# Attention scores in 64 x 64 quarters of the array, keys of the second batch prepared earlier in the step, and averages of v by TensorE

## The chip, the cores and the metric

The kernel runs on one core of a Trainium2 chip. The metric is the time of one execution in microseconds (us) on the device. One execution was also profiled; its trace gives the span from the first to the last instruction and every row shown below. The engines are called as the profile calls them: PE is TensorE's products and PEld its loads of the stationary operand, DVE is VectorE, ACT ScalarE, POOL GpSimd, and SP the engine that issues the DMA transfers.

## What is computed

Three parts stand one behind the other. All of it is float32.

```python
# attention: 2 batches, 8 heads, 768 positions, head size 64, block 32, window 16
k_sum = k.reshape(B, H, 24, 32, D).max(axis=3)
v_sum = v.reshape(B, H, 24, 32, D).mean(axis=3)
mask_l = abs(pos[:, None] - pos[None, :]) < 16
scores = concat(where(mask_l, scale * q @ k.T, -1e9), scale * q @ k_sum.T + log(32))
a = softmax(scores)
x = a @ concat(v, v_sum)
# dense MLP, 1536 tokens: 512 -> 2048 -> 512
h = x @ w_in
x = (h * sigmoid(h)) @ w_out
# top-1 mixture of 8 experts, 512 -> 1024 -> 512, capacity 384
out[i] = gate[i] * (relu(x[i] @ w1[e]) @ w2[e])
```

## The kernel before

The order of the instructions on every engine is the order in which the code is written; nothing reorders it.

**Units.** The attention is cut into 24 units of 256 queries and one pair of heads: four pairs per block of queries (`NPAIR` = 4), three blocks per batch, so twelve units per batch (`NPB`). A window of 96 keys (`WL`) and the 24 block keys make 120 columns (`WK`) for each group of 64 queries (`QB`), and a unit has four such groups (`UB`).

**Step.** `attn_step(n)` issues one step, in which several units are at different stages: maxima of unit n-1 (`s_max`, DVE), product with v of unit n-3 (`a_mm`, PE), transposes of P of unit n-2 (`p_mm`, PE), exponentials of n-1 (`s_exp`, ACT), transposes of queries of n+1 (`q_mm`, PE), copies of the attention's output of n-3 (`x_hi` on ACT, `x_lo` on DVE), copies out of the transposes (`p_ev`, `q_ev`), normalisation of n-1 (`s_norm`, DVE, then POOL), and at the end the scores of unit n (`s_mm`, PE). From unit 7 on a step begins with the MLP's first product for an earlier block (`l1`, L451), and from unit 9 it also has a second product (`l2_to`, L481) ahead of the scores. Pieces of the conversion of the MLP's weights (`conv_part`: three operations on DVE, a cast on ACT at L436, a subtraction on POOL at L437) stand between the stages.

**Scores before.** The queries of a unit lie transposed in `qt`. `q_ev` (L287) copies them with four ACT copies of 64 x 128 into `qbd`, a block-diagonal tile (two heads, each 64 rows by 64 columns, zero elsewhere), which POOL clears once at the start (L129). `s_mm` (L294) then needs four products, one for each group of 64 queries, which use the whole array and give 128 rows: 64 queries of one head above 64 of the other.

**Keys.** `k_prep(b, p)` transposes the keys of a pair of heads (L242) into two PSUM banks, `kA` and `kB`, ACT copies the windows out of them into `kwin` (L257, L261), and DVE takes the maxima of blocks of 32 (L263). It runs for the first batch ahead of the first scores (steps -1 to 2), and for the second in steps 11 to 14, behind the second product of the MLP and directly ahead of the scores.

**Averages of v.** For the first batch TensorE makes them: `vsum_mm(0)` multiplies v by a matrix `avg` of 1/32 (L207), behind the first scores, and ACT copies the result to `vsum` (L211), from where DMAs put rows of it to each unit's v (L343). For the second batch they are summed in steps 3 to 11: eight loads (`load_vs`), additions on POOL for three of them (L219, L221), reductions on DVE for five (L223), two more to bring parts together, and eight small DMAs that place them (`vs_place`).

**PSUM.** Of the eight banks, the pool "att" has four, which `qt`, `kA`, `kB`, `sc`, `pt`, `av` and `vsp` take in turn; "h" (first product) and "x2" (second) have two each.

## Time and profile before

| what | value |
|---|---|
| median of 3 runs | 515.15 us (514.3 to 515.69) |
| the profiled execution | 514.7 us |
| span of its trace | 513.0 us |
| mean granted TensorE clock | 0.976 of full |
| PE busy | 479.9 us |
| DVE busy | 296.0 us |
| ACT busy | 247.4 us |
| POOL busy | 135.6 us |

A median is compared with a median; the rows of the trace belong to the one profiled execution and are taken against its span of 513.0 us, which lies 1.7 us under that execution's time. Busy times of engines lie beside each other and do not add up.

### The profile page before, as it was taken

Reading aid. Unit: us, or ns where it says so; the run is one execution under the profiler, and the core shown is the slowest. Engines: PE = TensorE matmul, PEld = TensorE weight load, DVE = VectorE, ACT = ScalarE, POOL = GpSimd, SP = SyncE. Lnnn points to the kernel's source line nnn. Section 1 sums busy time; section 2 is a strip of 40 time slices with the busy share of each in tenths; the row PEclk is TensorE's granted clock in tenths of the full one; section 3 lists DMA queues with packets and bytes.
Section 4 is the critical chain, followed back from the end, with each engine's and each line's share of the span. In section 5 each row is a group of like instructions: output and inputs, shape, how many; then the busy total and the mean of one; then the engine's idle time right before and its main releaser. Section 6 shows DMA issues by size and latency. Waiting matters only on the chain. (4 is left out here: it accounts for less than half of the span.)

```text
span 513.0 us, 9798 instructions
## 1 busy us (share of the span) xinstructions
PE 479.9 (94%) x3318; PEld 416.8 (81%) x3318; DVE 296.0 (58%) x857; ACT 247.4 (48%) x746; POOL 135.6 (26%) x154
## 2 busy tenths in 40 slices
PE   4877989999999999999999999999999998999994
PEld 2366878898988899999998998888878897988852
DVE  1277886765545988666666434556666673445500
ACT  4478868977753533333333333334543344346511
POOL 6027753362433532222112100112412012101011
PEclk9957989999999999999999999999999999999998
DMA  8479777246301677655540000128251367718470
GB/s 204 101 201 278 187 193 200 65 121 165 75 2 42 173 211 215 217 156 149 151 177 0 1 1 0 44 74 318 78 191 55 89 204 226 251 45 288 151 236 16
DMA packets 82055, 71.15 MB, mean 139 GB/s; under 512 B 36822, under 2 KB 66776, under 8 KB 81984
## 3 DMA queue, kind: packets, MB, share of 16 engines
q1 hardware_dynamic: 80288, 66.17, 44.6%
q0 software_dynamic: 1696, 4.13, 2.1%
q8 instruction: 33, 0.54, 0.4%
q14 instruction: 38, 0.31, 0.2%
HBM read 55.38 MB, written 15.09 MB: 137 GB/s over the span
## 5 line engine op out<-in xcount | busy, mean ns | idle before, releaser
L451 PE MATMUL hp<-xT,w 128*128 128x256 f32 x1152 | 156.8, 286 | 2.3 <-ACT w L436 1.4
L451 PEld LDWEIGHTS hp<-xT,w 128*128 128x128 f32 x1152 | 149.6, 192 | 8.1 <-ACT w L436 1.6
L481 PE MATMUL x<-w,g 128*128 128x512 f32 x576 | 151.6, 398 | 1.1 <-ACT rows L487 1.1
L481 PEld LDWEIGHTS x<-w,g 128*128 128x128 f32 x576 | 101.8, 189 | 20.2 <-issue 2.1
L454 ACT ACTIVATE u<-hp 128x256 f32<-128x256 f32 x96 | 37.0, 385 | 98.3 <-PE hp L451 94.8
L459 DVE SCALAR_TENSOR_TENSOR u<-u,hp 128x256 f32<-128x256 f32 x96 | 40.2, 418 | 63.9 <-ACT u L454 63.6
L463 ACT CAST g<-u 128x256 fp32r<-128x256 f32 x96 | 39.4, 410 | 60.3 <-DVE u L459 60.0
L437 POOL TENSOR_TENSOR w<-cv,w 128x512 fp32r<-128x512 f32 x32 | 42.8, 1339 | 95.9 <-ACT w L436 95.8
L791 PE MATMUL hp<-XT,H 128*128 128x384 f32 (+1 forms) x288 | 48.8, 320 | 2.2 <-ACTq L948 1.4
L791 PEld LDWEIGHTS hp<-XT,H 128*128 128x128 f32 x288 | 45.8, 188 | 4.6 <-ACTq L948 1.8
L757 PE MATMUL y<-H,gh 128*128 128x512 f32 x192 | 48.6, 397 | 0.0
L467 DVE TENSOR_TENSOR g<-u,g 128x256 fp32r<-128x256 f32 x72 | 31.4, 437 | 27.6 <-ACT g L463 17.0
L326 POOL TENSOR_TENSOR P<-P,rs 128x480 f32<-128x480 f32 x24 | 26.3, 1095 | 60.6 <-DVE rs L325 53.8
L757 PEld LDWEIGHTS y<-H,gh 128*128 128x128 f32 x192 | 35.1, 188 | 7.2 <-issue 0.4
L736 DVE TENSOR_TENSOR H<-R,H 128x1024 fp32r<-128x1024 f32 x24 | 29.4, 1224 | 17.2 <-ACT H L735 17.2
L568 POOL DMA_INDIRECT disp<-rows,di x12 | 13.4, 1119 | 97.5 <-DVE rows L566 58.7
L316 ACT ACTIVATE P<-P,nm 128x120 f32<-128x120 f32 x96 | 36.6, 384 | 4.2 <-DVE nm L305 4.1
L796 ACT ACTIVATE gh<-hp 128x384 fp32r<-128x384 f32 (+1 forms) x24 | 10.9, 456 | 47.2 <-PE hp L791 46.7
L294 PEld LDWEIGHTS sc<-kwin,qbd 128*128 128x128 f32 x192 | 28.3, 220 | 4.8 <-DVE nm L305 1.7
L294 PE MATMUL sc<-kwin,qbd 128*128 128x120 f32 x192 | 30.2, 308 | 2.0 <-DVE nm L305 1.0
L735 ACT CAST H<-R 128x1024 fp32r<-128x1024 f32 x27 | 28.1, 1042 | 2.2 <-SPq L948 1.6
L765 POOL DMA_INDIRECT out_dram<-ys,aux x8 | 9.8, 1231 | 72.2 <-ACT ys L764 36.5
(175 smaller groups left out, 576.7 us busy)
## 6 DMA issues: line engine op xcount, KB each, us to landing
R<-in_moe_w_dram SPq DMA_DIRECT2D x34, 512.0 KB
ri<-in_moe_w_in_dram SPq DMA_DIRECT2D x16, 512.0 KB
ro<-in_moe_w_out_dram SPq DMA_DIRECT2D x16, 512.0 KB
disp<-zt SPq DMA_DIRECT2D x24, 260.0 KB
q_n<-in_q_dram SPq DMA_DIRECT2D x48, 64.0 KB
k_n<-in_k_dram SPq DMA_DIRECT2D x16, 192.0 KB
out_dram<-zt SPq DMA_DIRECT2D x12, 256.0 KB
rows<-in_moe_w_dram SPq DMA_DIRECT2D x6, 512.0 KB
```

The costliest lines, as they stand in the source:

```text
L294: PE.matmul(sc[:, i, :], lhsT=qbd[u % 2][:, i, :], rhs=kwin[p][:, i0 + i, :], start=True, stop=True)
L316: ACT.activation(P[:, i, :], P[:, i, :], AF.Exp, bias=nm[:, i : i + 1], scale=-1.0, accum_out=sm[:, i : i + 1])
L437: POOL.tensor_sub(w[:, 2 * j + 1, :], t, w[:, 2 * j, :].bitcast(F32))
L451: PE.matmul(hp, lhsT=w[:, a, c], rhs=x[:, b_, kk, :], start=n == 0, stop=n == 3 * KT - 1)
L454: ACT.activation(u, hp, AF.Tanh, scale=0.5)
L459: DVE.scalar_tensor_tensor(out=u, in0=u, scalar=1.0, in1=hp_t.pop(s), op0=ALU.add, op1=ALU.mult)
L463: ACT.copy(gt[s][:, 0, :], u_t[s])
L467: eng.tensor_sub(gt[s][:, 1, :], u_t.pop(s), gt[s][:, 0, :].bitcast(F32))
L481: PE.matmul(x2[blk][t], lhsT=gh[:, a, c], rhs=w[:, b_, :], start=first and n == 0, stop=last and n == 2)
L736: (eng or DVE).tensor_sub(h[:, 1], r, h[:, 0].bitcast(F32))
L757: PE.matmul(y, lhsT=gh[:, a, c], rhs=mx[1, f // 2][:, b_, DM * (f % 2) : DM * (f % 2) + DM], start=first and n == 0, stop=last and n == 2,)
L791: PE.matmul(hp, lhsT=h1(f // 2, a, kk, c), rhs=XT[:, b_, kk, 0:N], start=n == 0, stop=n == 3 * KT - 1)
```

## The change

Four things change.

1. *Scores.* `s_mm` has eight products in place of four. Each multiplies the 64 rows of one head by 64 queries, and so takes one quarter of the array: the head (h) chooses the upper or lower 64 rows, and the even or odd group of queries (e) the columns. The two heads write to two PSUM banks. `qbd` goes; `q_ev` is one copy of 128 x 256 to `qT`. The mask has three groups of columns instead of six. `load_q` reads runs of 256 bytes instead of 512.
2. *A bank of its own.* `qa` is one of the four "att" banks for good: the transposed queries lie in its first half, the product with v in its second. Three are left to take turns for scores (two of them at a time), transposes of P, and the keys of the second batch.
3. *Keys.* `kB` begins at 384 instead of 512, so no window lies across both banks: seven transposes instead of six, four ACT copies instead of eight, and the maxima are issued ahead of the copies. The first batch's keys use the banks "x2"; the second batch's preparation moves ahead of the second product.
4. *Averages of v.* The first batch's product moves from behind the scores of unit 0 to behind those of unit 1, takes a bank of "h", and is copied out by DVE; its loads move behind those of the third keys, and `vs_rows` one step later. The second batch's eight loads, POOL and DVE sums and placing DMAs go. Four loads take their place, each of a pair of heads, and `vs_mm` with six products of 24 x 128 in steps 12, 13, 15 and 16, copied out by DVE.

Constants that only the router needs are set later on POOL (`late_constants`), and the first weights' conversion is begun in steps 3 and 5 instead of 2 and 4.

```diff
+    qa = psum.tile([128, 2, 256], F32, tag="att", bufs=4, name="qa")
...
-    qbd = [ap1.tile([128, UB, 128], F32, name=f"qbd{i}") for i in range(2)]
-    for t in qbd:
-        POOL.memset(t, 0.0)
...
+    VR = S // 128
+    avg6 = ap1.tile([128, VR, NSUM], F32, name="avg6")
+    POOL.memset(avg6, 1.0 / BLK)
+    for sgn in (1, -1):
+        POOL.affine_select(
+            out=avg6,
+            in_=avg6,
+            pattern=[[sgn, VR], [-sgn * BLK, NSUM]],
+            compare_op=ALU.is_ge,
+            fill=0.0,
+            base=0 if sgn == 1 else BLK - 1,
+            channel_multiplier=sgn * VR,
+        )
+    late_constants()
...
-            SP.dma_start(out=t[:, h], in_=q[b, 2 * p + h, s0 : s0 + TB, :].rearrange("(p r) d -> p r d", r=2))
+            SP.dma_start(out=t[:, :, h], in_=q[b, 2 * p + h, s0 : s0 + TB, :].rearrange("(t p) d -> p t d", p=128))
...
-    NVP = 4
-
-    def load_vs(b, i):
-        g, j = divmod(i, NVP)
-        n = BLK // NVP
-        t = stage.tile([96, n, D], F32, tag="vs", bufs=2, name="vs_n")
+    def load_vs(b, p):
+        t = stage.tile([128, 2, VR, D], F32, tag="vs", bufs=2, name="vs_n")
         SP.dma_start(
-            out=t,
-            in_=v[b, 4 * g : 4 * g + 4].rearrange("h (n t) d -> (h n) t d", t=BLK)[:, j * n : j * n + n, :],
+            out=t.rearrange("p h r d -> p h (r d)"),
+            in_=v[b, 2 * p : 2 * p + 2].rearrange("h (p r) d -> p h (r d)", r=VR),
         )
-        vs_n[b, i] = t
+        vs_n[b, p] = t
...
-        ps = psum.tile([128, H, D], F32, tag="att", bufs=4, name="vsp")
+        ps = psum.tile([128, H, D], F32, tag="h", bufs=2, name="vsp")
...
-        ACT.copy(vsum[WL:WK], ps[WL:WK])
-
-    def vs_reduce(b, i):
-        g, j = divmod(i, NVP)
-        t = vs_n.pop((b, i))
-        if i < 3:
-            w = BLK // NVP // 2
-            while w > 1:
-                POOL.tensor_add(t[:, 0:w, :], t[:, 0:w, :], t[:, w : 2 * w, :])
-                w //= 2
-            POOL.tensor_add(vs_p[g][:, j, :], t[:, 0, :], t[:, 1, :])
-        else:
-            DVE.reduce_sum(vs_p[g][:, j, :], t.rearrange("p t d -> p d t"), axis=AX.X)
-        if j == NVP - 1:
-            DVE.reduce_sum(vs_t[g], vs_p[g].rearrange("p j d -> p d j"), axis=AX.X)
-            DVE.tensor_scalar_mul(vs_t[g], vs_t[g], 1.0 / BLK)
-
-    def vs_place():
-        for g in range(2):
-            for h in range(4):
-                SP.dma_start(out=vsum[WL:WK, 4 * g + h, :], in_=vs_t[g][NSUM * h : NSUM * h + NSUM, :])
+        DVE.tensor_copy(vsum[WL:WK], ps[WL:WK])
+
+    def vs_mm(b, p):
+
+        t = vs_n.pop((b, p))
+        ps = psum.tile([128, 2, D], F32, tag="h", bufs=2, name="vs2")
+        for r in range(VR):
+            PE.matmul(ps[WL:WK], lhsT=avg6[:, r, :], rhs=t[:, :, r, :], start=r == 0, stop=r == VR - 1)
+        DVE.tensor_copy(vsum[WL:WK, 2 * p : 2 * p + 2, :], ps[WL:WK])
...
-        c0 = 512
-        pa = psum.tile([128, 512], F32, tag="att", bufs=4, name="kA")
-        pb = psum.tile([128, 512], F32, tag="att", bufs=4, name="kB")
-        for i in range(S // 128):
-            dst = pa[:, 128 * i : 128 * i + 128] if i < 4 else pb[:, 128 * i - 512 : 128 * i - 384]
-            PE.transpose(dst, t[:, i].rearrange("p h d -> p (h d)"), ident)
...
+        parts = []
+        for name, lo, hi, w0, w1_, c in (("kA", 0, 512, 0, 7, 0), ("kB", 384, S, 7, NQB, 512)):
+
+            tag, bufs = ("x2", 2) if b == 0 else ("att", 4)
+            ps = psum.tile([128, 512], F32, tag=tag, bufs=bufs, name=name)
+            for i in range(lo // 128, hi // 128):
+                PE.transpose(ps[:, 128 * i - lo : 128 * i - lo + 128], t[:, i].rearrange("p h d -> p (h d)"), ident)
+            parts.append((ps, lo, hi, w0, w1_, c))
+        for ps, lo, hi, w0, w1_, c in parts:
             DVE.reduce_max(
-                ks[:, lo // BLK : hi // BLK],
-                src[:, 0 : hi - lo].rearrange("p (n t) -> p n t", t=BLK),
+                ks[:, c // BLK : hi // BLK],
+                ps[:, c - lo : hi - lo].rearrange("p (n t) -> p n t", t=BLK),
                 axis=AX.X,
             )
+            i = w0
+            while i < w1_:
+                n = 1
+                while i + n < w1_ and wstart(i + n) == wstart(i) + n * QB:
+                    n += 1
+                a = wstart(i) - lo
+                assert a >= 0 and a + (n - 1) * QB + WL <= hi - lo
+                sl = ps[:, a : a + 1]
+                ACT.copy(
+                    kw[:, i : i + n, 0:WL],
+                    bass.AP(tensor=sl.tensor, offset=sl.offset, ap=[list(sl.ap[0]), [QB, n], [1, WL]]),
+                )
+                i += n
...
-        qt = psum.tile([128, TB], F32, tag="att", bufs=4, name="qt")
+        qt = qa[:, 0]
         t = q_n.pop(u)
-        for h in range(2):
-            PE.transpose(qt[:, 128 * h : 128 * h + 128], t[:, h].rearrange("p r d -> p (r d)"), ident)
+        for i in range(2):
+            PE.transpose(qt[:, 128 * i : 128 * i + 128], t[:, i].rearrange("p h d -> p (h d)"), ident)
         qt_t[u] = qt
 
     def q_ev(u):
-        qt = qt_t.pop(u)
-        for h in range(2):
-            dst = qbd[u % 2][64 * h : 64 * h + 64, :, 64 * h : 64 * h + 64].rearrange("p i (c r) -> p i c r", r=2)
-            for r in range(2):
-
-                src = qt[64 * r : 64 * r + 64, 128 * h : 128 * h + 128]
-                ACT.copy(dst[:, :, :, r], src.rearrange("p (i c) -> p i c", c=QB // 2))
+        q_t[u] = ap2.tile([128, TB], F32, tag="qT", name="qT")
+        ACT.copy(q_t[u], qt_t.pop(u))
...
     def s_mm(u):
         T, p = divmod(u, NPAIR)
         i0 = (T % NTH) * UB
-        sc = psum.tile([128, UB, WK], F32, tag="att", bufs=4, name="sc")
-        for i in range(UB):
-            PE.matmul(sc[:, i, :], lhsT=qbd[u % 2][:, i, :], rhs=kwin[p][:, i0 + i, :], start=True, stop=True)
+
+        sc = [psum.tile([128, UB // 2, WK], F32, tag="att", bufs=4, name="sc") for _ in range(2)]
+        qT = q_t.pop(u)
+        for j in range(UB // 2):
+            for h in range(2):
+                w = slice(D * h, D * h + D)
+                for e in range(2):
+                    i = 2 * j + e
+                    PE.matmul(
+                        sc[h][QB * e : QB * e + QB, j, :],
+                        lhsT=qT[w, QB * i : QB * i + QB],
+                        rhs=kwin[p][w, i0 + i, :],
+                        start=True,
+                        stop=True,
+                    )
         sc_t[u] = sc
...
-        av = psum.tile([128, TB], F32, tag="att", bufs=4, name="av")
+        av = qa[:, 1]
...
-        if n > 1 and (n - 1) % NPB == 0 and n - 1 < NU:
-            vs_place()
         on(p_mm, n - 2)
         conv_part()
         on(g_mul, s, NS)
         on(load_v, n - 1)
-        on(vs_rows, n - 1)
         on(s_exp, n - 1)
         conv_part()
         on(q_mm, n + 1)
         on(x_hi, n - 3)
-        if n == 0:
-            for T in range(NTH):
-                load_vp(0, T)
+        b, r = divmod(n + 1, NPB)
+        if 0 < b < B and r < NPAIR:
+
+            k_prep(b, r)
+        for p, (_, nu) in enumerate(VS_STEPS):
+            if n == nu:
+                vs_mm(1, p)
         l2_to(s - 2)
+        on(vs_rows, n - 2)
         on(p_ev, n - 2)
         on(q_ev, n + 1)
         on(s_norm, n - 1)
@@ -1071,32 +1077,36 @@
         if b < B and r < NPAIR:
             load_k(b, r)
         conv_part()
-        b, r = divmod(n + 8, NPB)
-        if 0 < b < B and r < 2 * NVP:
-            vs_reduce(b, r)
         on(x_lo, n - 3)
         b, r = divmod(n + 1, NPB)
-        if 0 <= b < B and r < NPAIR:
+        if b == 0 and r < NPAIR:
             k_prep(b, r)
         on(g_hi, s, NS)
         if n in (4, 5):
             load_raw()
             load_raw()
-        b, r = divmod(n + 9, NPB)
-        if 0 < b < B and r < 2 * NVP:
-            load_vs(b, r)
+        for p, (nl, _) in enumerate(VS_STEPS):
+            if n == nl:
+                load_vs(1, p)
         on(g_lo, s, NS)
         on(s_mm, n)
         if n == 0:
+            for T in range(NTH):
+                load_vp(0, T)
+        if n == 1:
             vsum_mm(0)
 
     NS = len(steps)
+
+
+    VS_STEPS = ((NPB - 4, NPB), (NPB - 3, NPB + 1), (NPB + 1, NPB + 3), (NPB + 2, NPB + 4))
+    assert B == 2 and len(VS_STEPS) == NPAIR
     fills = []
 
     for n in range(-2, NS + 2 + LEAD):
         s = n - LEAD
         if s < 0:
-            if n in (2, 4):
+            if n in (3, 5):
                 conv_to(n // 2)
             attn_step(n)
             continue
```

The first place is TensorE at the start of the program, from the first scores (`sc` of unit 0) to the third. `qt` and `qa` are transposed queries, `kA` and `kB` transposed keys, `vsp` the first batch's averages of v, `pt` transposes of P, `av` the product with v. Before:

```order
L294 MATMUL sc<-kwin_144,qbd_148 128x120 x4
L207 MATMUL vsp<-vp_n,avg 24x512 x6
L277 MATMUL qt<-ident,q_n 128x128 x2
L242 MATMUL kA<-ident,k_n 128x128 x4
L242 MATMUL kB<-ident,k_n 128x128 x2
L294 MATMUL sc<-kwin_145,qbd_149 128x120 x4
L332 MATMUL pt<-ident,P 120x128 x4
L277 MATMUL qt<-ident,q_n 128x128 x2
L242 MATMUL kA<-ident,k_n 128x128 x4
L242 MATMUL kB<-ident,k_n 128x128 x2
L294 MATMUL sc<-kwin_146,qbd_148 128x120 x4
```

And with the change, on the same engine and stretch:

```order
L291 MATMUL sc<-kwin_126,qT 64x120 x8
L273 MATMUL qa<-ident,q_n 128x128 x2
L243 MATMUL kA<-ident,k_n 128x128 x4
L243 MATMUL kB<-ident,k_n 128x128 x3
L291 MATMUL sc<-kwin_127,qT 64x120 x8
L218 MATMUL vsp<-vp_n,avg 24x512 x6
L336 MATMUL pt<-ident,P 120x128 x4
L273 MATMUL qa<-ident,q_n 128x128 x2
L243 MATMUL kA<-ident,k_n 128x128 x4
L243 MATMUL kB<-ident,k_n 128x128 x3
L291 MATMUL sc<-kwin_128,qT 64x120 x8
```

The averages have moved from ahead of the second unit's queries, keys and scores to behind them, and stand directly ahead of the first transposes of P.

The second place is ACT from the second unit's keys to the first exponentials and the next queries. `kwin` is where the key windows go, `P` the exponentials. Before:

```order
L257 COPY kwin_145<-kB 128x2x96
L261 COPY kwin_145<-kB 128x96
L211 COPY vsum<-vsp 24x512
L316 ACTIVATE P,sm<-P,nm 128x120 x4
L287 COPY qbd_148<-qt 64x4x32 x4
```

With the change:

```order
L278 COPY qT<-qa 128x256
L259 COPY kwin_127<-kA 128x96
L259 COPY kwin_127<-kA 128x6x96
L259 COPY kwin_127<-kB 128x4x96
L259 COPY kwin_127<-kB 128x96
L320 ACTIVATE P,sm<-P,nm 128x120 x4
```

The copy of the averages no longer stands ahead of the first exponentials on this engine.

The third place is TensorE in step 12, a unit with keys of the second batch: `hp` is the MLP's first product, `x` its second, `vs` the averages of the second batch. Before:

```order
L451 MATMUL hp<-xT,w 128x256 x12
L356 MATMUL av<-PT,v_n 64x64 x8
L332 MATMUL pt<-ident,P 120x128 x4
L277 MATMUL qt<-ident,q_n 128x128 x2
L481 MATMUL x_875<-w,g 128x512 x3
L481 MATMUL x_876<-w,g 128x512 x3
L242 MATMUL kA<-ident,k_n 128x128 x4
L242 MATMUL kB<-ident,k_n 128x128 x2
L294 MATMUL sc<-kwin_144,qbd_148 128x120 x4
```

With the change:

```order
L455 MATMUL hp<-xT,w 128x256 x12
L360 MATMUL qa<-PT,v_n 64x64 x8
L336 MATMUL pt<-ident,P 120x128 x4
L273 MATMUL qa<-ident,q_n 128x128 x2
L243 MATMUL kA<-ident,k_n 128x128 x4
L243 MATMUL kB<-ident,k_n 128x128 x3
L229 MATMUL vs_1128<-vs_n,avg_135 24x128 x6
L485 MATMUL x_830<-w,g 128x512 x3
L485 MATMUL x_831<-w,g 128x512 x3
L291 MATMUL sc<-kwin_126,qT 64x120 x8
```

Keys' transposes now stand ahead of the second product, and six products of averages between the two.

## Rows read from the trace of the kernel before

**Rows 1.** Page, part 1: busy time, share of the span, instructions.

```profile
PE 479.9 (94%) x3318; PEld 416.8 (81%) x3318; DVE 296.0 (58%) x857; ACT 247.4 (48%) x746; POOL 135.6 (26%) x154
```

**Rows 2.** Stretches: length; PE, PEld, DVE, ACT, POOL busy; clock, DMA share, GB/s.

```profile
0.00:21.00 21.00, 13.68 (x37) 6.21 (x37) 3.47 (x14) 6.39 (x25) 7.96 (x32) 1.00 0.73 165
21.00:50.40 29.40, 20.91 (x157) 17.79 (x157) 19.81 (x72) 24.74 (x100) 14.07 (x15) 0.73 0.80 216
50.40:74.40 24.00, 20.90 (x183) 18.47 (x182) 20.79 (x69) 17.59 (x67) 14.51 (x16) 0.90 0.76 193
74.40:108.90 34.50, 34.13 (x314) 30.50 (x314) 24.69 (x97) 28.96 (x126) 14.00 (x18) 1.00 0.52 126
108.90:152.90 44.00, 44.00 (x414) 39.69 (x413) 23.30 (x109) 31.42 (x126) 17.41 (x20) 1.00 0.39 94
```

**Rows 3.** Timeline of PE: start, duration, instruction, count; one unit.

```profile
108.93 1.67 PE L451 MATMUL hp<-xT,w 128*128 128x256 f32 x12
...
111.76 1.62 PE L481 MATMUL x<-w,g 128*128 128x512 f32 x6
...
113.23 1.05 PE L294 MATMUL sc<-kwin,qbd 128*128 128x120 f32 x8
...
114.03 0.36 PE L451 MATMUL hp<-xT,w 128*128 128x256 f32 x1
```

**Rows 4.** Timeline around the router's logits.

```profile
312.53 0.16 PEld L508 LDWEIGHTS lt<-xt,wg 128*32 128x32 f32 x8
...
312.53 0.64 PE L508 MATMUL lt<-xt,wg 128*32 128x256 f32 x8
...
313.10 0.50 PE L481 MATMUL x<-w,g 128*128 128x512 f32 x1
```

**Rows 5.** Timeline of PEld: two loads of the first batch's averages.

```profile
17.85 0.10 PEld L207 LDWEIGHTS vsp<-vp_n,avg 128*24 128x24 f32 x1 [0.33 <-issue]
18.28 0.10 PEld L207 LDWEIGHTS vsp<-vp_n,avg 128*24 128x24 f32 x1 [0.33 <-issue]
```

**Rows 6.** Timeline of a unit with keys of the second batch.

```profile
78.67 0.60 PE L242 MATMUL kA<-ident,k_n 128*128 128x128 f32 x4
...
79.11 0.38 PE L242 MATMUL kB<-ident,k_n 128*128 128x128 f32 x2
...
79.33 0.24 ACT L261 COPY kwin<-kA 128x96 f32<-128x96 f32 x1
```

**Rows 7.** Timeline of the start, ACT, PE and DVE; idle before and releaser in brackets.

```profile
8.29 1.14 ACT L287 COPY qbd<-qt 64x128 f32<-64x128 f32 x4 [2.83 <-POOL qbd L129]
...
11.98 0.54 PE L294 MATMUL sc<-kwin,qbd 128*128 128x120 f32 x1
...
13.95 7.07 PE L207 MATMUL vsp<-vp_n,avg 128*24 128x512 f32 x12
...
21.05 0.58 ACT L211 COPY vsum<-vsp 24x512 f32<-24x512 f32 x1 [7.46 <-PE vsp L207]
...
24.89 0.65 PE L332 MATMUL pt<-ident,P 128*120 128x128 f32 x4 [1.88 <-POOL P L326]
...
29.23 1.64 PE L294 MATMUL sc<-kwin,qbd 128*128 128x120 f32 x6 [0.82 <-ACT PT L338]
...
30.06 0.43 DVE L422 TENSOR_SCALAR cv<-ri 128x512 uint32<-128x512 uint32 x1 [2.40 <-DMA ri<-in_moe_w_in_dram]
```

**Rows 8.** Groups, 50.4 to 74.4: count, busy us, mean ns, idle before.

```profile
L451 PE MATMUL hp<-xT,w 128*128 128x256 f32 x49 | 8.3, 320 | 2.3 <-ACT w L436 1.4 <-POOL w L437 0.8
...
L287 ACT COPY qbd<-qt 64x128 f32<-64x128 f32 x17 | 4.6, 272 | 0.3
...
L223 DVE TENSOR_REDUCE vs_p<-vs_n 96x64 f32<-96x512 f32 x4 | 4.2, 1060 | 0.0
...
L369 ACT CAST xT<-av 128x256 fp32r<-128x256 f32 x4 | 1.4, 353 | 0.0
```

**Rows 9.** Timeline of DVE ahead of the first MLP product.

```profile
49.16 1.50 DVE L324 TENSOR_SCALAR rs<-sm 128x4 f32<-128x4 f32 x1 [1.08 <-ACT P L316]
```

More of the change, by code (lines that the diff above doesn't have):

```diff
@@ L106, in big_tile @@
         return big.tile(shape, dtype, tag="big", name=name)
-    mask = ap1.tile([128, 6, WK], F32, name="mask")
+    mask = ap1.tile([128, 3, WK], F32, name="mask")
     POOL.memset(mask, 0.0)
-    for h in range(2):
-        m = mask[64 * h : 64 * h + 64]
-        for lo, hi, off in ((0, 1, 0), (1, 5, WIN), (5, 6, 2 * WIN)):
+    for e, parts in enumerate((((0, 1, 0), (1, 3, WIN)), ((0, 2, WIN), (2, 3, 2 * WIN)))):
+        m = mask[QB * e : QB * e + QB]
+        for lo, hi, off in parts:
             for sgn in (1, -1):
@@ L126 @@
     kwin = [ap1.tile([128, NQB, WK], F32, name=f"kwin{p}") for p in range(NPAIR)]
-    qbd = [ap1.tile([128, UB, 128], F32, name=f"qbd{i}") for i in range(2)]
-    for t in qbd:
-        POOL.memset(t, 0.0)
     vsum = ap1.tile([128, H, D], F32, name="vsum")
-    vs_p = [ap1.tile([96, 4, D], F32, name=f"vs_p{i}") for i in range(2)]
-    vs_t = [ap1.tile([96, D], F32, name=f"vs_t{i}") for i in range(2)]
     avg = ap1.tile([128, NTH, NSUM], F32, name="avg")
@@ L145 @@
         )
+    VR = S // 128
+    avg6 = ap1.tile([128, VR, NSUM], F32, name="avg6")
+    POOL.memset(avg6, 1.0 / BLK)
+    for sgn in (1, -1):
+        POOL.affine_select(
+            out=avg6,
[7 more added lines that the diff above has]
+    late_constants()
     q_n, v_n, k_n, vs_n = {}, {}, {}, {}
@@ L278, in q_mm @@
         qt_t[u] = qt
     def q_ev(u):
-        qt = qt_t.pop(u)
-        for h in range(2):
-            dst = qbd[u % 2][64 * h : 64 * h + 64, :, 64 * h : 64 * h + 64].rearrange("p i (c r) -> p i c r", r=2)
-            for r in range(2):
-                src = qt[64 * r : 64 * r + 64, 128 * h : 128 * h + 128]
-                ACT.copy(dst[:, :, :, r], src.rearrange("p (i c) -> p i c", c=QB // 2))
+        q_t[u] = ap2.tile([128, TB], F32, tag="qT", name="qT")
+        ACT.copy(q_t[u], qt_t.pop(u))
@@ L303, in s_max @@
         nm = ap2.tile([128, UB], F32, tag="nm", name="nm")
-        for i in range(UB):
+        for g in range(UB):
+            h, j = divmod(g, UB // 2)
+            i = i0 + 2 * j
             DVE.tensor_tensor_reduce(
-                out=P[:, i, :], in0=sc[:, i, :], in1=mask[:, m0 + i, :], scale=-scale, scalar=3.0e38,
-                op0=ALU.add, op1=ALU.min, accum_out=nm[:, i : i + 1],
+                out=P[:, g, :], in0=sc[h][:, j, :], in1=mask[:, 0 if i == 0 else 2 if i == NQB - 2 else 1, :],
+                scale=-scale, scalar=3.0e38, op0=ALU.add, op1=ALU.min, accum_out=nm[:, g : g + 1],
             )
@@ L358, in a_mm @@
                     lhsT=vt[0:WK, i, h, :],
-                    rhs=ps[0:WK, i, 64 * h : 64 * h + 64],
+                    rhs=ps[0:WK, UB // 2 * h + i // 2, QB * (i % 2) : QB * (i % 2) + QB],
                     start=True,
```

41 lines of the change are left out of this document (10 added, 31 removed).

## The prediction

> **What bounds the kernel now.** I read the busy shares first: TensorE is busy 94% of the span [rows 1], so there is little idle time to win and whatever lengthens its own work counts. The second view, busy time by stretch, says where the rest lies [rows 2]. From 108.90 to 152.90 us TensorE is busy in every microsecond, from 74.40 to 108.90 in 34.13 of 34.50. In the first 21 us it is busy for only 13.68, and from 21.00 to 50.40, where the granted clock is 0.73 of full, for 20.91 of 29.40 us; from 50.40 to 74.40 it is 20.90 of 24.00 at 0.90. So the kernel has two regimes. Up to 74.4 us the chain of waits decides, and an instruction saved on another engine can shorten it. From 74.4 us TensorE decides, and only TensorE's own instructions count. Everything behind the attention (from 152.9 us) is the same code before and after, so I let it shift as a whole.
>
> Nothing here is below about 0.3% of the time, 1.5 us, which is what a measurement of this kernel can tell from no change. The profiled execution took 514.7 us, a span of 513.0 and 1.7 around it; the median shown is 515.15, 0.45 above. I work out a difference on the span and take it off the median.
>
> **A unit where TensorE decides** [rows 3]. One step runs from the first product of one unit at 108.93 us to the next at 114.03: 5.10 us. Its scores take from 113.23 to 114.03, 0.80 us for eight passes, 0.10 each.
>
> *Scores in quarters.* Eight passes through the whole array become sixteen through a quarter each. If four quarters run abreast, that is four rounds of 0.10 us and a changeover into and out of the tiled form. No quarter-array product stands in the trace. The nearest row is the router's logits [rows 4]: eight passes of 256 columns through column tiles of 32 take from 312.53 us to the next product at 313.10, 0.57 us. At 0.43 us for a pass of 512 columns (below), two rounds of 256 are 0.43, so the eight ran four abreast, and the changeover behind them is 0.14; I allow nearly as much ahead of it, 0.11 (between 0 and 0.14), so 0.25. The quarters then cost 4 x 0.10 + 0.25 = 0.65 us, 0.15 less per unit. If only two run abreast it is 0.80 + 0.25 = 1.05, 0.25 more; one after another, 1.60 + 0.25 = 1.85, 1.05 more. I take four abreast, as the nearest row has it, and keep the others as rivals, since that row has column tiles alone and the quarters are split by rows too.
>
> All eight weight loads of that logits block, those of the second round too, begin and end between 312.53 and 312.69 us, while the first four passes stand on the same rows of the array [rows 4]. [...]
>
> *Averages of v by TensorE.* Four new groups of six products of 24 by 128. The passes of the first batch's same product are 0.43 us apart for 512 columns (17.85, 18.28), two passes to a product [rows 5]; 128 columns are a quarter, 0.107, so twelve passes are 1.28 us, and a changeover of 0.25 makes 1.53. Four of them: +6.1 us in units 12, 13, 15 and 16, where TensorE decides, so nothing covers them. From below, only what idle TensorE time those units have can hide them, at most the 0.37 us that 74.40 to 108.90 leaves [rows 2]; from above, two changeovers each, +7.1. Their copy out is a DVE copy of 24 x 128, off the path: DVE is busy 24.69 of these 34.50 us.
>
> *Keys.* A transpose takes 0.11 us (four from 78.67 to 79.11) [rows 6]. Seven in place of six is +0.11 per preparation, +0.44 for the four of the second batch. Before, such a unit ends with a wait: scores cannot begin before the keys' copies, which start at 79.33 us, after the transposes. The six units from one first product at 74.40 to another at 108.90 take 34.5 us [rows 2]; six at 5.10 are 30.6, and 24 transposes 2.6, which leaves 1.3 us of waits in four units. With the transposes ahead of the second product, its 1.47 us (111.76 to 113.23 [rows 3]) cover the maxima and the copies. I take 0.9 of the 1.3 as won; bounds 0 and 1.3, less another 0.5 if the new second half of the keys holds back a scores bank, since three banks now rotate where four did.
>
> *TensorE's regime in sum,* units 11 to 23: averages +6.1, transposes +0.4, scores 13 x -0.15 = -2.0, waits -0.9: **+3.6 us**.
>
> **The first 21 us and the filling** [rows 7]. Before, GpSimd clears the two block-diagonal tiles, the first copy of queries waits 2.83 us for that and starts at 8.29, and the first scores run at 11.98. The clearing goes, and a query copy is one of 0.353 us, as the cast of the same shape [rows 8], where four of 0.27, 1.1 us, stood. The copies of keys are four instead of eight. I put the first scores 2 us earlier, near 10.
>
> More is in the averages of the first batch. They occupy TensorE from 13.95 to 21.0 us. ScalarE sits idle 7.46 us for their copy out at 21.05 and the first exponentials stand behind that copy, though the scores they need were begun at 11.98; the normalisation and the first transposes of P, 24.89, follow. In the change the product is behind the second unit's scores, and DVE copies it out, behind the first normalisation. So exponentials and normalisation run beside it, and the transposes of P start as it ends, near 21.1: 3.8 us earlier. The scores of the third unit, 29.23 us, waited on ScalarE's copies of P (released by that copy). They need only free banks once their keys are ready a step earlier; transposes of P, of queries and 7 of keys then come to 1.7 us, so near 22.8: **-6.5 us**. What is late next are the first MLP weights: DVE waits 2.40 us for their load until 30.06. That load is behind the same or more issues on SP's queue, as the averages' three loads are now behind the third keys; nothing makes it come sooner.
>
> From there to the first MLP product (50.40 us) are 21.2 us, in which the first weights are converted. ScalarE has 0.7 us less per unit, and the 1.5 us that DVE took over a sum of four columns at 49.16, beside GpSimd's adds for v, goes with those adds [rows 9]. That could give 4 more. But DMA is busy 0.80 of this stretch at 216 GB/s [rows 2], and the same weights must come in a shorter time; and queries and averages of attention now share a bank, so each unit's product with v waits for the copy out of the one before. I take -1, between +2.5 (the weights hold it back) and -3.5. **Up to 50.4: -7.5 us**, bounds -10 and -4.
>
> **50.4 to 74.4 us** [rows 8]. Four units need 4 x 3.63 (5.10 less the second product's 1.47) and two second products 1.47 each: 17.5 us of 24.0. What holds it are the conversions: TensorE waits 2.3 us here for weights, from ScalarE and GpSimd, which wait for DVE. DVE loses four reductions of 1.06, 4.2 us, and ScalarE 17 query copies of 0.272 less four of 0.353, 3.2 us; scores 4 x -0.15 = -0.6. I take **-3.3**, half of what the six and a half us of slack allow; bounds -1 (if DMA is what is late) and -5.
>
> **Sum:** -7.5 - 3.3 + 3.6 = -7.2 us; 515.15 - 7.2 = **508.0**, and 505.8 for a span that was 513.0. Its own range by the bounds, not all at one end: 505 to 511.5.
>
> **Rivals.** (1) *Two quarters abreast.* [...] 0.40 us more than forecast in the 17 units from 7 on, +6.8: about **515**, no change. (2) *Quarters one after another.* A block of 1.85, 1.20 over the forecast in 17 units: +20.4, about **528.5**, slower. It decides, and the kernel becomes slower, once a scores block costs more than its 0.65 by 7.2 / 17 = 0.42, that is above 1.07 us. (3) *The early gain is not passed on.* The chain to 50.4 is set by the arrival of weights at 0.80 DMA share, and the shared bank makes waits: -2 up to 50.4 and -1 to 74.4, with +3.6 behind: **515.8**, no change to slightly slower. For it speaks the DMA share, against it that in the first 21 us DMA is only at 0.73, and the 2.40 us wait is one wait in 29. (4) *The averages' product costs nearly nothing,* because their loads and passes fit under waits of units with keys: +1.5 in place of 6.1: about **503.5**. Against it stands TensorE's 34.13 busy of 34.50.
>
> **Chances.** Forecast 0.54, (1) 0.17, (2) 0.06, (3) 0.12, (4) 0.11. The range drops (2) and the outer tails: 503.0 to 516.5. Faster by over 0.3% (under 513.6): the forecast and (4), with a few hundredths of (1) and (3): 0.70. Within: most of (1) and some of (3): 0.12. Slower (over 516.7): (2), part of (1) and (3), and the unknown cost of the shared bank: 0.18.
>
> **What the profile after would show.** A steady unit without keys of 4.95 us, with its scores in 0.65 (right), in 1.05 (rival 1) or 1.85 (rival 2). The averages' twelve passes in about 1.5 us in four units (rival 4 if their step is not longer). First transposes of P near 21, third scores near 23; if those are right and the first MLP product is still at 50, rival 3. First MLP product near 43 and the step at 74.4 near 63.6; attention's end near 145.7. I would be wrong above all if the scores block is longer than the 0.80 it replaces, or if the three rotating banks make TensorE wait in each unit: then the busy share from 74 us on falls below what it was.

## The result: slower, and the profile after

The changed kernel takes 520.36 us (median of 4 runs, 519.13 to 521.86) where the kernel before, run beside it, takes 514.75; the ratio is 1.0115, 95% interval 1.0082 to 1.0148. The forecast was 508.0 us in 503.0 to 516.5. The profiled execution took 519.13 us, with a span of 517.4 where before it was 513.0. Part 1 of its page, and the view of stretches (columns as in [rows 2]), over the same five stretches:

```profile
PE 478.4 (92%) x3566; PEld 409.2 (79%) x3566; DVE 293.3 (57%) x853; ACT 226.6 (44%) x641; POOL 127.0 (25%) x142
```

```profile
0.00:21.00 21.00, 14.26 (x77) 7.83 (x77) 5.99 (x21) 7.73 (x24) 6.87 (x30) 1.00 0.90 190
21.00:50.40 29.40, 19.56 (x231) 15.88 (x231) 17.88 (x81) 18.59 (x72) 11.31 (x9) 0.71 0.77 190
50.40:74.40 24.00, 20.48 (x228) 16.56 (x227) 19.43 (x66) 16.57 (x62) 14.48 (x16) 1.00 0.86 228
74.40:108.90 34.50, 33.40 (x347) 27.12 (x346) 19.97 (x80) 20.14 (x77) 11.56 (x15) 1.00 0.59 144
108.90:152.90 44.00, 44.00 (x478) 36.79 (x476) 23.75 (x108) 25.28 (x104) 16.70 (x20) 1.00 0.30 66
```

TensorE has 1.5 us less to do than in [rows 1] and the span is 4.4 us longer, so the kernel waits more. The first row of [rows 2] had 13.68 us of TensorE where 14.26 stand now; 50.4 to 74.4 has a granted clock of 1.00 instead of 0.90. From 108.90 on TensorE is busy throughout, as before. Only the row from 74.40 on shows a loss, TensorE busy for 33.40 us where it was 34.13: one of the signs of being wrong that the prediction had named, but 0.7 us, where the span is 4.4 us longer.

To see where the loss is I laid the two timelines of TensorE side by side, one product against the same product:

| start of, us | before | after | difference |
|---|---|---|---|
| third scores | 29.23 | 22.54 | -6.7 |
| first MLP product (unit 7) | 50.44 | 45.16 | -5.3 |
| first product of unit 11 | 74.36 | 66.71 | -7.7 |
| first product of unit 17 | 108.93 | 108.58 | -0.3 |
| an MLP product behind the attention | 148.86 | 147.53 | -1.3 |
| last second product ahead of the first branch below | 457.89 | 457.43 | -0.5 |
| second product behind that branch | 466.10 | 467.57 | +1.5 |
| first transposes of the last expert part | 491.76 | 496.27 | +4.5 |

The attention ends 1.3 us earlier, not 7.2, and then 5.8 us are lost where the diff changes nothing: 0.8 between 361 and 375 us, the rest behind two branches of the experts (places at which a condition decides which block of instructions is next). Timelines of the kernel before and then of the changed one, TensorE's first products behind the two branches and, between them, ScalarE's first instruction behind the first (L735 and L739 are the same line):

```profile
463.17 3.09 PE L791 MATMUL hp<-XT,H 128*128 128x256 f32 x24 [0.82 <-ACTq L959]
...
463.73 1.05 ACT L735 CAST H<-R 128x1024 fp32r<-128x1024 f32 x1 [0.65 <-ACTq L959]
...
487.98 3.86 PE L837 MATMUL hp<-R,few 128*64 128x256 f32 x32 [1.09 <-ACTq L959]
```

```profile
464.64 3.08 PE L795 MATMUL hp<-XT,H 128*128 128x256 f32 x24 [2.76 <-ACTq L963]
...
465.20 1.05 ACT L739 CAST H<-R 128x1024 fp32r<-128x1024 f32 x1 [2.59 <-ACTq L963]
...
490.91 5.43 PE L841 MATMUL hp<-R,few 128*64 128x256 f32 x32 [2.57 <-ACTq L963]
```

In the changed kernel ScalarE stands idle for 2.59 us where it stood for 0.65, TensorE 2.76 instead of 0.82 and then 2.57 instead of 1.09. The releaser is each time ScalarE's sequencer, at the line of the `with` that holds the experts' conditions (L959, L963). The same 32 products then take 5.43 us instead of 3.86. The stretches around that second branch, before and after, show the clock:

```profile
485.90:488.00 2.10, 1.01 (x6) 0.51 (x4) 0.41 (x4) 1.38 (x2) 0.32 (x1) 1.00 0.04 8
488.00:491.80 3.80, 3.80 (x33) 2.32 (x33) 0.00 (x0) 0.38 (x1) 0.65 (x1) 1.00 0.86 230
```

```profile
487.40:490.90 3.50, 0.94 (x4) 0.41 (x3) 0.41 (x4) 1.38 (x2) 0.97 (x1) 1.00 0.34 85
490.90:496.30 5.40, 5.39 (x33) 4.66 (x33) 0.00 (x0) 0.38 (x1) 0.97 (x1) 0.68 0.95 333
```

From 487.40 to 490.90 TensorE is busy for 0.94 us of 3.50, and the granted clock of the block behind it is 0.68, where it was 1.00. So one longer wait cost 1.5 us, and the block behind it, at that clock, another 1.6.

What the prediction named for the attention itself is there. A steady unit, from first product to first product:

```profile
113.58 1.70 PE L455 MATMUL hp<-xT,w 128*128 128x256 f32 x12
...
116.45 1.64 PE L485 MATMUL x<-w,g 128*128 128x512 f32 x6
...
118.03 0.64 PE L291 MATMUL sc<-kwin,qT 64*64 64x120 f32 x16
...
118.60 0.39 PE L455 MATMUL hp<-xT,w 128*128 128x256 f32 x1
```

The loads of its scores, in the timeline of PEld:

```profile
118.02 0.41 PEld L291 LDWEIGHTS sc<-kwin,qT 64*64 64x64 f32 x16 [0.37 <-issue]
```

The unit is 5.02 us (113.58 to 118.60), where it was 5.10. The scores block is 0.57 us where eight passes took 0.80 [rows 3]; the second product ahead of it takes 1.58 instead of 1.47. From unit 17 to 23 the lead over the kernel before grows by 0.10 to 0.13 a unit, apart from one unit that took 5.33 us before. And a unit with averages of v:

```profile
105.00 1.49 PE L229 MATMUL vs<-vs_n,avg 128*24 128x128 f32 x12
...
106.42 1.66 PE L485 MATMUL x<-w,g 128*128 128x512 f32 x6
...
108.58 0.39 PE L455 MATMUL hp<-xT,w 128*128 128x256 f32 x1
```

The averages take 1.42 us up to the second product, and the unit 6.61 in all (from 101.97), 1.6 over a steady one. At the start, a row each of PE, DVE and PE:

```profile
22.54 0.64 PE L291 MATMUL sc<-kwin,qT 64*64 64x120 f32 x16
...
29.43 0.43 DVE L426 TENSOR_SCALAR cv<-ri 128x512 uint32<-128x512 uint32 x1 [3.98 <-DMA ri<-in_moe_w_in_dram]
...
31.84 0.91 PE L360 MATMUL qa<-PT,v_n 120*64 120x64 f32 x12 [5.44 <-DVE xT L378]
```

The third scores stand at 22.54. VectorE then waits 3.98 us for the first MLP weights (2.40 in [rows 7]), and the second product with v waits 5.4 us for VectorE's copy out of the first, which is queued behind that conversion.

### The profile page after: what moved, and what is told of

Its sections match the earlier page's. It is cut to its first block, busy times and chain, and to the rows that moved or that the text cites. A ratio compares the mean times of both kernels' runs of the same rounds, so it can differ in the third digit from the quotient of the medians.

```text
span 517.4 us, 10197 instructions
## 1 busy us (share of the span) xinstructions
PE 478.4 (92%) x3566; PEld 409.2 (79%) x3566; DVE 293.3 (57%) x853; ACT 226.6 (44%) x641; POOL 127.0 (25%) x142
## 5 line engine op out<-in xcount | busy, mean ns | idle before, releaser
L471 DVE TENSOR_TENSOR g<-u,g 128x256 fp32r<-128x256 f32 x72 | 33.9, 471 | 27.6 <-ACT g L467 16.5
L739 ACT CAST H<-R 128x1024 fp32r<-128x1024 f32 x27 | 28.1, 1042 | 3.4 <-ACTq L963 2.6
L360 PE MATMUL qa<-PT,v_n 120*64 120x64 f32 x384 | 17.8, 239 | 11.9 <-DVE xT L378 6.1
L769 POOL DMA_INDIRECT out_dram<-ys,aux x8 | 8.6, 1070 | 75.3 <-ACT ys L768 50.2
L360 PEld LDWEIGHTS qa<-PT,v_n 120*64 120x64 f32 x384 | 14.4, 148 | 15.9 <-DVE xT L378 6.7
```

The costliest lines, as they stand in the source:

```text
L360: PE.matmul(av[64 * h : 64 * h + 64, QB * i : QB * i + QB], lhsT=vt[0:WK, i, h, :], rhs=ps[0:WK, UB // 2 * h + i // 2, QB * (i % 2) : QB * ...
L471: eng.tensor_sub(gt[s][:, 1, :], u_t.pop(s), gt[s][:, 0, :].bitcast(F32))
```

## Experiments

Two theories stood for the tail: **A**, ScalarE waits for its own code behind a branch, and whether it does depends on where the code lies; **B**, data of the experts or later work. The changed kernel has 117 instructions fewer on ScalarE ahead of the experts (685 before, 568 after, counted in the two programs). That their place can matter was an assumption of mine, which nothing had shown yet. Runs below are compared with the kernel before on the same chip; its median was 513.8 to 515.3.

**after_placed: the code back in its place,** by 117 copies of one element on ScalarE.

```diff
+            for _ in range(min(3, 117 - npad[0]) if s >= 30 else 0):
+                ACT.copy(padt[0:1, npad[0] : npad[0] + 1], ident[0:1, 0:1])
+                npad[0] += 1
```

> [...] Theory A (the tail's loss is loading of ScalarE's code behind taken branches, which depends on where the code falls): TensorE's waits at the two branches to the last expert stages fall from 2.76 and 2.57 us to about 0.8 and 1.1, the granted clock no longer falls behind the second, and the tail gives back about 5 us: 514 to 515 us in all. Rival B (the tail waits for data of the experts, or for work that ScalarE does later): waits within 0.5 us of the change's, 519 to 521 us.

513.19 us, ratio 0.9967 (0.9949 to 0.9985). TensorE behind the two branches:

```profile
461.05 3.09 PE L796 MATMUL hp<-XT,H 128*128 128x256 f32 x24 [0.82 <-ACTq L964]
...
485.85 3.76 PE L842 MATMUL hp<-R,few 128*64 128x256 f32 x32 [1.09 <-ACTq L964]
```

0.82 and 1.09 us, as in the kernel before, and the 32 products in 3.76. 117 instructions that do nothing make the change 7 us faster.

**before_shifted: the opposite, on the kernel before.** It gets 139 copies, which with its 685 instructions are 824, 256 more than the change's 568. That a place 256 instructions further on gives the change's waits was an assumption of mine too.

> [...] Theory A: the waits of 2.8 and 2.6 us at the last branches and the fall of the clock appear here too, 4 to 6 us more than before, 519 to 521 us. Rival B: no wait moves, 514.5 to 515.5 us.

522.35 us, ratio 1.0145 (1.0114 to 1.0175).

```profile
464.51 4.39 PE L792 MATMUL hp<-XT,H 128*128 128x256 f32 x24 [2.58 <-ACTq L960]
...
492.07 3.74 PE L838 MATMUL hp<-R,few 128*64 128x256 f32 x32 [2.57 <-DMA Xg<-disp]
```

Waits of 2.58 and 2.57, where the change has 2.76 and 2.57; this time the first block is the longer one (4.39 us instead of 3.09), and the second, in a stretch with a granted clock of 1.00 (485 to 497 us), takes 3.74. The tail's loss is there without any of the change: 4.5 us in this trace, by the two waits and the first block. The profiled execution (518.57 us) was the shortest of five; what the others lost beyond that, no trace shows. The second wait is put down to a DMA here, where it was ScalarE's sequencer in the change; that DMA is issued 0.12 us after the wait begins, here and in after_placed alike, so it is not what differs.

**after_other: a place between** (53 instead of 117). If the place decides in steps, each wait has one of the values seen so far.

> The change with 53 copies added on ScalarE instead of 117, so its code of the experts stands 64 instructions ahead of where the kernel before has it. [...] Rival: waits grow with the shift by degrees, half way at 1.8 and 1.8.

515.47 us, ratio 1.0035 (1.0010 to 1.0060).

```profile
460.35 3.09 PE L796 MATMUL hp<-XT,H 128*128 128x256 f32 x24 [0.82 <-ACTq L964]
...
486.42 5.43 PE L842 MATMUL hp<-R,few 128*64 128x256 f32 x32 [2.58 <-DMA Xg<-disp]
```

The first wait is that of before, the second that of the change, to 0.01 us: no value between. Where the code lies decides, as theory A has it, and by steps.

The traces also show instructions being moved. They list DMA packets of kind "instruction". The view of DMA from the start of TensorE's first wait to its end, in the change and then in after_placed:

```profile
q14 instruction: 1, 0.01, 1.3%
```

```profile
DMA packets 0, 0.00 MB, mean 0 GB/s; under 512 B 0, under 2 KB 0, under 8 KB 0
```

Each of the five long waits of the change, before_shifted and after_other has one such packet, of 8192 bytes, that starts 1.0 us after the wait begins and ends 0.3 to 0.7 us later. The short waits at the first branch have none, in before and in every version with the code at its place; those at the second have at most one, which starts in their last 0.1 us. For which engine a packet is, the trace doesn't say.

All further versions have ScalarE's code at the place of before (their waits at the two branches are 0.82 and 1.09 to 1.20 us), so they compare with after_placed, 0.9967. They ran on several chips, and one kernel's ratio differed by 0.006 from chip to chip (rows1 below): smaller differences between versions from two chips are not to be read.

**early: first MLP weights loaded in step 1.** The theory (C) was that the early gain is lost to those weights; the rival (D), that DMA decides.

```diff
+        if n == 1:
+            load_raw()
+            load_raw()
         b, r = divmod(n + 3 if n + 3 >= NPB else n + 2, NPB)
```

> The change with ScalarE's code placed as in the kernel before, and the loads of the first MLP weights issued in step 1 instead of with the first conversion in step 3. Theory C (the early gain is given back because VectorE stands 3.98 us on the first weights, and what TensorE needs next is queued behind that): the wait falls under 1 us, the second product with v comes from 31.84 to about 28, the first MLP product from 45.17 to 41.5 to 43, and the time to 2 to 3.5 us under the change with its code placed alone. Rival D (the first stretch is bound by what DMA can bring, so an earlier load only delays others): first MLP product within 1 us of 45.17 and no gain.

513.20 us, 0.9966 (0.9947 to 0.9984): no gain. VectorE's wait for the first weights went, and the third keys, which now stood behind a megabyte of weights, were late by as much (TensorE's waits for keys, first 46 us; 2.7 us in two waits in after_placed):

```profile
PE kA L244 <- DMA k_n<-in_k_dram: 6.4, 2, 4.7
```

**early2: only the first of the two, behind the keys.**

```diff
+        if n == 1:
+            load_raw()
```

> The change with ScalarE's code placed, and one load alone, that of the first half block of MLP weights, issued at the end of step 1, behind the fourth keys, instead of with the first conversion in step 3. Theory C: VectorE's wait for it, 3.7 us, falls under 1, nothing that the early units need is late by more than 1 us, and the first MLP product comes 2 to 3 us earlier. Rival D (DMA decides the stretch): what is behind it on the queue is as much later, first MLP product within 1 us, time the same as with the code placed alone, 513.2.

512.43 us, 0.9973 (0.9949 to 0.9997). First MLP product at 41.88 us, unit 11 at 64.64, 2.3 us ahead of after_placed, and lost again in unit 11, in a wait of 2.2 us ahead of the product with v and slower products behind it. Theory C has its mechanism and not its gain.

**extra: two loads that nobody reads.**

```diff
+        if n in (2, 5):
+            SP.dma_start(out=spare, in_=wo32[512 + 128 * n : 640 + 128 * n, :])
```

> The change with ScalarE's code placed, and two loads of 0.52 MB that nobody reads, in steps 2 and 5. All versions so far reach the first product of unit 14 at 88.7 to 91.0 us with 17.7 MB brought by then and DMA busy 0.80 to 0.83, whatever TensorE had saved earlier. Theory D (DMA decides up to there): 1.05 MB at 200 GB/s put it 4 to 5 us later, and 515.5 to 518 us in all. Rival K (chains between engines decide, DMA has 0.19 of its time left): at most 1.5 us later, 513 to 514.5.

514.79 us, 0.9994 (0.9971 to 1.0018), some 1.5 us over after_placed. Stretches up to the first product of unit 14, of extra and of after_placed:

```profile
0.00:88.52 88.52, 67.80 (x677) 51.40 (x678) 50.74 (x197) 52.08 (x191) 36.78 (x59) 0.92 0.85 212
```

```profile
0.00:88.69 88.69, 65.88 (x677) 49.49 (x678) 50.66 (x197) 52.12 (x191) 36.72 (x59) 0.92 0.81 200
```

Unit 14 begins at 88.52 and 88.69 us. A megabyte more fitted under a DMA share of 0.85, so that the share of 0.81 was no bound by itself. But the profiled execution (513.23 us) was the shortest of ten, and the median is 3.0 us over rows1, which ran beside it. So D falls as I had put it, 4 to 5 us, and a smaller part for DMA is not excluded.

**rows1 and rows1_again: early2, and rows of averages a step earlier.**

```diff
-        on(vs_rows, n - 2)
+        if n == 2:
+            vs_rows(0)
+        if n >= 2:
+            on(vs_rows, n - 1)
```

> The change with ScalarE's code placed, the first load of MLP weights in step 1, and the rows of averages written to v one step earlier, as in the kernel before. Without the last, the earlier weights gained 2.4 us up to unit 11 and lost it there in a wait of 2.2 us for the product with v. Theory L (that wait was for the rows of averages, which stood on the queue behind half a megabyte of weights): the wait goes, unit 14 at 86.5 to 87.5 us, 510.5 to 511.5. Theory D: another wait takes its place, unit 14 at 88.5 to 89.5, 512 to 513.5.

> The version with the rows of averages a step earlier and the first weights in step 1, again, beside the others on one chip. If the first timing holds: 511 to 512.3 us, ratio to before 0.990 to 0.994. If it was the few runs: 512.7 to 513.5, as with the code placed alone.

511.75 us, 0.9907 (0.9873 to 0.9940) in 4 runs, then 511.98, 0.9963 (0.9944 to 0.9982) in 11. The median hardly moved; the kernel before beside it did, 515.31 and then 513.80 on another chip. With eleven runs the version is no faster than after_placed by its ratio. The wait in unit 11 went, and in rows1_again TensorE waited 3.5 us for ScalarE's cast of weights instead.

**avtwo: two buffers for the product with v.**

```diff
-        av = qa[:, 1]
+        av = qa[:, u % 2]
```

(and the transposed queries in the free half of the bank of `hp`)

> The change with ScalarE's code placed as before, both halves of the qa bank taking the product with v by turns, and the transposed queries in the free half of the bank of the MLP's first product. Theory G (TensorE waits because one half bank holds the product with v, so each product waits for VectorE's copy out of the one before): the waits ahead of the product with v in units 8, 9, 11 and 12 (0.36, 0.30, 0.91, 1.10 us in the change) go, and the attention ends 2 to 3 us earlier than with the code placed alone. The 5.4 us ahead of the second product with v become a wait of the transposes behind it, since the normalisation stands behind the same conversion. Rival H (these are waits for the softmax or the conversions that would only show elsewhere): end of the attention within 0.5 us.

513.16 us, 0.9976 (0.9956 to 0.9995). TensorE's waits, 45 to 112 us:

```profile
PE hp L278 <- DVE u L470: 3.4, 2, 2.9
PE qa L365 <- ACT g L474: 0.3, 1, 0.3
```

The waits ahead of the product with v are down to 0.3 us, as G has it, but the queries' transposes, now tied to the bank of `hp`, waited 3.4. No gain, and no clean test, since my placing of the queries made the new wait.

**oldavg2, oldavg3: the second batch's averages by GpSimd and VectorE again,** placed in step 14 and in step 13.

```diff
-        for p, (_, nu) in enumerate(VS_STEPS):
-            if n == nu:
-                vs_mm(1, p)
...
+        b, r = divmod(n + 8, NPB)
+        if 0 < b < B and r < 2 * NVP:
+            vs_reduce(b, r)
```

> The change with ScalarE's code placed, and the second batch's averages of v made as before, by GpSimd and VectorE, placed one step later than in the kernel before. Theory E: units 12, 13, 15 and 16 are 1.6 us shorter, 6.3 in all; the conversions of weights come 2 to 4 us later again up to 74 us; net 2.5 to 4.5 us under 513.2. Rival F: no difference.

> The change with ScalarE's code placed and the second batch's averages of v made by GpSimd and VectorE, and placed in step 13, behind the last rows of the first batch (a step earlier than in the version that waited 3.4 us for them). Theory D: units 12 and 13 gain nothing, since DMA has to bring the same, units 15 and 16 gain 1.6 us each: unit 17 begins 2 to 3 us earlier than with the code placed alone, 510 to 511.5 us. Theory E as first put (6.3 us saved in four units): 507 to 509. Rival F (VectorE's reductions take it all back): 513.

518.68 us, 1.0098 (1.0071 to 1.0125), and 517.31, 1.0029 (1.0009 to 1.0049). (A first attempt, oldavg, placed them while the last unit of the first batch still needed its own, so the later parts work on other values; its 545.18 us compares with nothing.) Both are slower than after_placed, which none of my theories had (oldavg3 is 5.6 us over rows1, which ran beside it). TensorE in oldavg3, 45 to 112 us:

```profile
PE qa L366 <- DVE xT L384: 4.4, 4, 3.0
```

The reductions of 1.06 us stand on VectorE ahead of the copy out of the product with v, and with one buffer for that product TensorE waits for it. The 6.4 us that v's averages cost TensorE in the change are gone here, and the time is no shorter.

**combo: oldavg3, early2 and rows1 together.**

> All of it together: ScalarE's code placed, averages of the second batch by GpSimd and VectorE, first weights in step 1, rows a step earlier. If the parts add up as theory D has it (nothing before unit 14, 3 us in units 15 and 16), 509 to 511.5 us; if the early parts add to that, 507.5 to 509; if VectorE and GpSimd take it back, 513.

513.33 us, 0.9937 (0.9910 to 0.9963) in 9 runs, between oldavg3 and rows1 on the same chip. Against rows1 (0.9907), whose interval overlaps, GpSimd's and VectorE's averages cost 1.6 us by the medians, though TensorE waits for VectorE's copy here too (4.4 us).

**quarters: the kernel before, with the scores' part of the change alone.**

```diff
-            PE.matmul(sc[:, i, :], lhsT=qbd[u % 2][:, i, :], rhs=kwin[p][:, i0 + i, :], start=True, stop=True)
...
+                    PE.matmul(
+                        sc[h][QB * e : QB * e + QB, j, :],
+                        lhsT=qT[w, QB * i : QB * i + QB],
+                        rhs=kwin[p][w, i0 + i, :],
...
```

> The kernel before with the scores in quarters alone (one copy of queries, mask of three groups, loads of queries in runs of 256 bytes; four banks still taken in turn), ScalarE's code placed as before. Theory I (a unit saves 0.11 us where TensorE decides, and ScalarE's fewer copies help before that): steady unit 5.01 us instead of 5.12, attention's end 2 to 4 us earlier, 511 to 513 us. Rival J (five tiles a step in four banks make new waits): end of the attention no earlier, 514 to 516 us.

513.47 us, 0.9973 (0.9948 to 0.9998). A steady unit is 5.01 us here too. The scores alone win about what the whole change wins. The averages of the second batch are still made by GpSimd and VectorE there, and the four banks still taken in turn: the other three parts of the change together win nothing that shows.

**vsum_back: the first batch's averages where they were.**

```diff
         if n == 0:
-            for T in range(NTH):
-                load_vp(0, T)
-        if n == 1:
             vsum_mm(0)
```

(with its loads and ScalarE's copy as before)

> The change with ScalarE's code placed, and the first batch's averages as in the kernel before: product in step 0 behind the first scores, its loads ahead of the third keys, copied out by ScalarE. The prediction's step (the move is worth 6.5 us at the third scores, of which all but 1 to 2 is passed on): third scores at 29 us instead of 22.5, first MLP product 4 to 6 us later than with the code placed alone, 517 to 519 us. Rival M (the weights' arrival and conversion decide, so the move is passed on only in part): third scores 6 us later too, first MLP product 1 to 2.5 us later, 513.5 to 515.5.

511.80 us, 0.9954 (0.9932 to 0.9976), the lowest ratio of those with ten or more runs. TensorE from the averages to the third scores, and the second scores of the kernel before:

```profile
11.55 5.52 PE L219 MATMUL vsp<-vp_n,avg 128*24 128x512 f32 x12
17.00 0.44 PE L274 MATMUL qa<-ident,q_n 128*128 128x128 f32 x2
...
18.13 0.64 PE L292 MATMUL sc<-kwin,qT 64*64 64x120 f32 x16
...
22.74 1.08 PE L292 MATMUL sc<-kwin,qT 64*64 64x120 f32 x16
```

```profile
21.96 1.05 PE L294 MATMUL sc<-kwin,qbd 128*128 128x120 f32 x8
```

The third scores stand at 22.74 us, as early as with the move. The move wins nothing that shows.

**keys_back: the second batch's keys directly ahead of the scores.**

```diff
-        if 0 < b < B and r < NPAIR:
-
-            k_prep(b, r)
...
-        if b == 0 and r < NPAIR:
+        if 0 <= b < B and r < NPAIR:
             k_prep(b, r)
```

> The change with ScalarE's code placed, and the second batch's keys behind the second product, directly ahead of the scores, as in the kernel before, with seven transposes. The prediction's step (0.9 us of waits won in four units): 0.5 to 1.5 us later at unit 15, 513.7 to 514.7. Rival N (VectorE and ScalarE take keys no sooner, so no wait is won): within 0.5 us. Rival O (with three banks in turn, scores must wait for the keys' banks whole): each of the four units 1 us longer or more, 517.

519.97 us, 1.0108 (1.0072 to 1.0144). TensorE in unit 11:

```profile
71.79 0.60 PE L244 MATMUL kA<-ident,k_n 128*128 128x128 f32 x4
72.22 0.49 PE L244 MATMUL kB<-ident,k_n 128*128 128x128 f32 x3
72.64 0.42 PE L292 MATMUL sc<-kwin,qT 64*64 64x120 f32 x4
73.98 0.63 PE L292 MATMUL sc<-kwin,qT 64*64 64x120 f32 x12 [0.92 <-ACT kwin L260]
```

Scores begin behind the keys and stop for 0.92 us for the copies out of them (such waits come to 4.4 us in the four units); unit 17 begins at 114.53 instead of 107.75.

## Why the prediction was wrong

**"Everything behind the attention ... is the same code before and after, so I let it shift as a whole."** This is the step that failed. The same instructions lay at another place, the waits at two branches were 1.9 us longer for ScalarE and 1.5 for TensorE, and the granted clock behind one of them was 0.68 instead of 1.00. after_placed, after_other and before_shifted show it from both sides: 7 us by the medians; in the profiled execution 5.8, of which 5.0 are the two waits and the block at that clock and 0.8 stand ahead of them, unexplained. It turned a gain into a loss. Of the 12.4 us between the forecast and the median, this is 7.2; the other 5.2 are the attention's.

**The attention.** With the code placed, the change wins 1.9 us (0.9967), not 7.2. By terms:

- *Quarters:* the four quarters run abreast: from 118.02 to 118.10 us four passes are under way, and the 0.57 us of all sixteen exclude two abreast (0.80 without a changeover). The block and the 0.11 us ahead of it come to 0.68, where I had 0.65; forecast 0.15 a unit won, measured 0.10 to 0.13. Two of the four share their rows, and all sixteen loads begin and end between 118.02 and 118.43 us, while the block's products run (118.03 to 118.60), as the logits' loads did on shared rows [rows 4]. Rivals 1 and 2 are out.
- *Averages on TensorE:* forecast 1.53 a unit, measured 1.6; rival 4 is out. Whether they pay stays open: oldavg3 is slower without them, but combo hardly is, and quarters, without them, is as fast as the whole change.
- *Keys ahead of the second product:* I counted 0.9 us of 1.3 won. Unit 14 had hardly a wait to win (5.80 before, 5.81 after). Unit 13 takes 7.38 us, 5.8 without the averages' 1.6, where it took 6.16, so some 0.4 went there. Units 11 and 12 lost more than that in new waits ahead of the product with v (0.91 and 1.10 us in the profiled execution). With the other parts of the change the old place costs 7 us (keys_back); that the third bank is the reason is argued, not tested.
- *Up to the third scores:* forecast -6.5, measured -6.7, and the cause was wrong, so that the number was luck: vsum_back has -6.5 without the averages' move. There the first scores begin 1.4 us earlier (10.54) and take 1.0 us less, the averages take 5.52 us where they took 7.07, and from the second scores to the third there are 4.6 us instead of 7.3. ScalarE, on which [rows 7] has the third scores wait, has fewer copies in that last part; quarters, which has the fewer copies of queries but not of keys, has the third scores at 24.03.
- *From there to unit 11:* forecast -10.8 at unit 11. Three profiles of the same code up to there (after, after_placed, after_other) give -7.7, -7.5 and -8.8, and at unit 17 -0.3, -1.2 and -3.1, so a single execution scatters by 2.7 us here and my terms were finer than that. The mean misses by 2.8 us at unit 11 and by 1.7 more up to unit 17. Rival 3 is what happened in part: the gain is there at 25 us and not passed on. Its cause as I had put it, DMA's rate, is not borne out at that size (extra).

What the missing 4.6 us at unit 17 wait for stays open. Each wait that I took away (weights, rows of averages, the single buffer) came back as another of about the same length; no single one decides.

## What to carry to other kernels

A kernel with branches can lose more by where its code lies (7 us here) than a change wins (1.9): compare the parts that the change doesn't touch first, product by product, and if they differ behind a branch, pad the engine that the wait names and time again. In a stretch where several chains are about as long, a saved wait is worth little until the next one is known; sum such a stretch with a discount, or test one part alone. And the price of a move depends on the others: with three banks in turn instead of four, the order of the keys was worth 7 us.

## What the runs showed of the hardware

Four 64 x 64 quarters with two on the same rows ran abreast: sixteen passes of 120 columns in 0.57 us. The product ahead of them took 1.58 us up to their start, where it took 1.47 ahead of scores on the whole array. TensorE's wait behind the first branch was 0.8 or 2.6 to 2.8 us, behind the second 1.1 to 1.2 or 2.6, and nothing between, by the place of ScalarE's code alone; in each of the five waits of 2.57 to 2.76 us a packet of instructions of 8192 bytes was moved. Behind these five the next products took longer three times (5.43 us twice, for 3.76 to 3.86, and 4.39 for 3.09) and twice not (3.08, 3.74). Over one block of 5.43 us the granted clock was 0.68, over those of 3.08 and 3.74 it was 1.00; over the others it is not shown.
